# Token-mixing sum of the first layer in two pieces, paired masks in one GpSimd instruction, and another order

## The chip, the cores and the metric

The kernel runs on one core of a Trainium2 chip. The metric is device time in microseconds, as the median of several executions. The profile is one such execution, taken by the hardware profiler.

A core has TensorE (PE; matmuls from SBUF into PSUM), VectorE (DVE), ScalarE (ACT), GpSimd (POOL, which works on SBUF alone here) and SyncE (SP, which issues all DMAs here). Each engine executes its own list of instructions in order and waits on semaphores for the others.

## What is computed

Two layers, each an attention block and a token-mixing MLP, over x of 2048 tokens by 512 channels in bf16. Attention has 32 heads of 16 channels, and a query sees itself and the 255 tokens before it. The MLP mixes over tokens: its sum over s has 2048 terms, its hidden size is 1792.

```python
def _A_ref(x, wqkv, wo):                       # H = 32, Dh = 16, W = 256
    q, k, v = qkv[0], qkv[1], qkv[2]           # from x @ wqkv
    scores = einsum("bhqd,bhkd->bhqk", q, k) * (Dh ** -0.5)
    mask = (i - j >= 0) & (i - j < W)
    p = softmax(where(mask, scores, -1e9))
    return einsum("bhqk,bhkd->bhqd", p, v) @ wo
def _B_ref(x, w1, b1, w2, b2):
    h = layernorm(x)
    u = gelu(einsum("bsd,sf->bdf", h, w1) + b1)
    return transpose(einsum("bdf,fs->bds", u, w2) + b2)
for layer in range(2):
    x = x + _A_ref(layernorm(x), wqkv, wo)
    x = x + _B_ref(layernorm(x), w1, b1, w2, b2)
```

## The kernel before, in words

**Graph and order.** The kernel first describes its work as a graph of some two thousand operations, each with an engine (or alternatives), the tiles it reads and writes, and a cost. Costs and priorities were used by a planner that isn't in the file; what is in the file is its outcome, the text `ORDER`. `replay` goes through it: each entry names the next operation and which of its alternatives (for an eviction, VectorE or ScalarE; for a product, GpSimd or VectorE) is taken. `ORDER` thereby fixes the list of every engine, of the DMA queue too, and which buffer each tile gets. `emit` then writes the instructions and the waits. So whenever the graph changes, a new `ORDER` is needed.

**Units.** A token block is 128 tokens (16 of them, t0 to t15); attention counts in blocks of 64. Channels are worked in four groups `o` of eight heads.

**Attention.** A layer's queries are cut into chunks (`CHUNKS`, L336). Layer 0 has chunks 0 and 1 of four 64-token blocks, then 2, 3 and 4 of eight; layer 1 has four chunks of eight. For every head group a plan (`attention_plan`) lists score steps: which key blocks against which queries, and which columns need a mask. A step is: score matmuls on PE (L673, into two PSUM pairs), two exponentials on ScalarE (L688, PSUM to `pt` in SBUF), the masks on GpSimd (L698, or L700 for a step of two head groups: a multiplication of `pt` by columns of the table `ldm`, seen as int32), and the product with V on PE (L716), which waits for masks. After a head group, VectorE transposes the sum (L736), takes reciprocals (L740), GpSimd or VectorE multiplies (L742), and VectorE transposes back (L747). In a full chunk of eight blocks there are five steps a head group with 1, 2, 2, 2 and 2 masks; a mask of two 64-blocks has 2 x 128 elements a partition, a mask of one has 2 x 64. GpSimd also does the layer norms' power (L485) and part of the K layout (L596).

**Between chunks.** `prepare` brings the layer norm, transposes and Q, K, V of the next 512 tokens. `wo_block` is the output projection of a finished chunk; the residual is added (L758), and the layer norm of those tokens follows (L469 to L492), which makes `xh` of these blocks.

**The MLP's first product** needs all 2048 tokens, so it can't be finished before attention; but part of the sum can be made as soon as some token blocks are normalised. `u_part(s0, s1)` sums over blocks s0 to s1-1: for each of 14 feature tiles of 128, a PSUM group of s1-s0 matmuls (each of 512 columns, L515), then an eviction into an fp32 array (`uA`, which lies in the places of w2b and uT). The first piece is copied there (L822 on VectorE or L824 on ScalarE), a later one is added on VectorE (L826). Every matmul of a piece waits for `xh` of its last block, s1-1 (L820). `PARTS` (L337) lists the pieces: in layer 0, blocks 0 to 3 after chunk 2, 4 to 7 after chunk 3 and 8 to 11 after chunk 4; in layer 1, 0 to 7 after chunk 2 (whose chunks are numbered from 0 too). `u_last` (L837) does the rest, blocks 12 to 15 in layer 0 and 8 to 15 in layer 1, adds what was kept (L848), and ScalarE makes the gelu (L852).

**Weights.** w1 comes through four buffers of 512 KB (`load_w1`, L772). A piece of n blocks loads 2048/n features in a buffer: four tiles for a piece of four blocks, seven for one of eight, with 14 and 28 DMAs of 128 KB. The loads of a piece are put behind the last scores of the chunk before it (`gate`). w2 follows through buffers of `pt` and w2b (L784).

**The MLP's second product** (`y_block`) is 14 matmuls a token block, then the residual (L864); layer 0's blocks are also filler for layer 1's first chunks. In-order PE runs score and value steps, with other matmuls (projections, `u_part`, `y_block`) in between as fillers.

Of the kernel before, what the change touches and what calls it, by code (L numbers as in the profile page):

```python
# [14 lines left out]
ORDER = (
    'c-qZYF^KEP86Mf=-',
    '8q;89q3>JDkh)<9jMR)6$&VzfC36Aph5u^Djaa(LWK(z4mh9#1va3<g%4af;KGFq2Yldwi&waC;lhQBEnK*8V2dqWY~ce3w#cttd+mMi-sW=TA',
    'phHEk7oWE{qz0b|NUkNA?$ljh9bvF5_m$s?}rGvn(I4`qbVll?{q`g-',
    '?_|nUDQY#iel9sb_ZS29uDDs81W$3Zsd6&o7}LuRaZStbu`YoIOW+*p68yo(`CG6x}K%m^>THew~hH+*WZUNX1k-',
    'NY%!CuT2)VT)>Lep!CqFa$t<wa^g-1Ot)=ViPQAklU#nbMDx!Iqn|sdn$3wyxn>^INa-',  # L20
    '3+nS}s;gX8)E^gvR5^csv%Ps;len1WePYX1Ck@@HYX^f;>0cMwZ>tG)-N1Gt-',
    '+?rItCX*Th<_Mk8t%8tmxxR2C#+Gm4CkZCkmOPt`0RZpC+>>w4PK7K=ujX>lCat%0R!wOHG$T&<!=Q5ubgL>E|c99a&(lp{H0OerkSZ;Xt|lB6',
    'oDEYs$LL8?zSy{)!&KQj!&v@BDW2SyYrUDq{2<JT?GlK~T^OOhnZx=vxMVXRb1=6hX{ab+rFCNm}-',
    '4sv_B++`V8=gof(1_OC3%MxS8g0VQ(HA(t*^d0`aqv)n>sv-w0Ih+L}F3U=!DvHcEciY-Vtja4HY^LMSyBOQ_?}w413@Gj49w8)(`ZUb*PPdcO',
    'n`RSZ)6Bb0s$0}c)5_Ob95+a<=G5UkCcn$-',
    'X<f1$$*%i;&98z*aE9Z!J<^qJdyx_=Bg7KLwb8w~xdGsHQ4|%m@OG5YQIr{XX+;ALd_|;n2b1qHk>vY(Syokb+36hS)#&!K<uZ=vkTX%FwB7c<',
    'Gfcfj;T-xmN)-;cQ}uAb2qPp(e64VLPpH5jIlp~R$b{fW2#V}}*&QIXU86NZt6{snZ1;NeS(eQynxUp`+rv($-',
    '9~x0+r^a90dApY6CoADu@MU5I@~x2fDdsEPOB+O6zv|U?t~n`CP+ufu`yOPPt#PX*Oe@jo2JR3><H#EB0y%>6&z7^U5m@2iGU_l5=ACTsz?#$o',
    'M_{E9r8w$YL&A)LL^BLMN<S)NOZlH*Ibt9ZZVzC#0sToI3J+?2%#=Qw^?@6>Ev04Py<#Pv57E61m2ydjkupszvfziSOJk!RaH_9>O8BpD5A?HM',
    'hi5X1);dbh#}gSk<|q*B2CjZ!z6K>>2)1TDQOWOqLzX{;-)8=7GJUD;wC4quS%U*5@iuCWSW79Jl%^DT@Q3!hmz3>lSRe%0ZlrDBP4`zLn-pI-',  # L30
    '@}KZEEchCk~Z*%&h;$IEX^cOhPvG^>V=UO7D=^I0Uev#_GZ|3-',
    'G(iK$RW;=z>3VUdb3$In_(zPe(aC3G?jsdY{inK>ZDl^{2{4sf{nG?Z5Uc_rH$TztIzB8yTVl3QWS*N>qcxrt<LhEbz>PoM9qfG;>2h)FvTjef',
    'rU{d8>V2p1O!b3Aw*n-Fn9ytZ(3DsS?q8)AV&9l6nt+UJm#6-n-',
    'UfE$$mL|2mI<IIC!z>13(?H>>p(EFV}O2jfOvnYX{#Kq;DlE%k<U&VZJr~411_ffn5LzHpIsR&`wqVgb3MeHj;GM-',
    '`?IHmV3r_?EW6~@g9wbccQozHyc?tHW{ePYNZ&4g80{yAsdWFqhHW|x7PzPFbBqP(CZ-~<9GP4q|<G+x`#vF8GMHB@-(G1A&W(;1!-',
    'x4sHXjXf7(mak=bdXK8Rks*#!21T+$XeQJS_at8UKcW@g*XECm*-',
    '7U(_VY0y?$t*Bm&0JS6u!@#e*^_mw&>XgWC7=^VWnlJ!F{^F)#7%sP4D3!JCIM%JbvhVJeaGCksFy7DS^A7u(DYe?L+pV={Ri!!}4~HYKI*OF(',
    'bUGY6lW`dSDp(pzrLWEx%VB@e@6RSm56HjUjfRu$bh6*GZnxL%ZV<|#^1Z<G2A&rrN#cFuiEg!;B+W2Mq9|!55E=sMk4(i#xW-',
    '+x5&J&zL!Z*v>q2^>$cm~I`io&u8(Jze5$k+|(9Mly$vemD?{<d+)F(m$QlY$wNMP4+Jfw6Dn68#&xgw0rkU0Gk0R-UI>-',
    'P$JBuSdy6d!~2I%(oKrnnBxtl0uy26fOSU5|Cs^gR!GfURR!A1rR!mgjXm3Ja!Eh=GI((n;{~u#X=ecDvo<<0F842>1IaI!OCE5=D2pSaLpLvK',  # L40
    'cEgW>h!2&Y7IIZ}R31%d$R$9J4$Zb3i14LT)vit;Qdvq75M*RjVO%SSl)@1l0E}M{yj3Slle=D=Gxb(9OO;ly3wdxk9g7$gzN&W^%uU2n%c=M9',
    'kPIPy0}eBIprCiL$$&W0VxdUL&?+;ZA!58s6_W+!&>~>oxr(a@|1Tw(Zy)XfVWbzYjgZ03n=X=&`ES7%?PinyJ7~63N%4dMxo+m2`$(2NjtRHy',
    'UTscnpobT6H8QO(t&LAn=1`Hk;}CVv*11l+gQWK`$k5wI;)EtH0^Yl;JR#ciRucAfP>HJCrv`hEc~rc~TR#u&D*&d$muI({?<!PKe3Oz$A&+Fb',
    'M0n0?i6T%d%|AR4w35%e4$bIaerxaz*ef18|1kS13$j=qH%)WBml-zuRy&{J~f_omaF_NX7Z&GAjO#R{r#f*X7e<`RsN5GAbRvu3kT1x|gp?xO',
    '8=O`L1&L#s6hP={OWF&Ol}1`IJiWSGn*kouLw*K1u>yuXJ246_*u+rxBco&l@jZ2T))vJcTU0PSO)f!Z{DeSG|nN@K8QMTg+ejl|DqU^n}E#>5',
    'CgYLr^@IPGFQyQ=d5SB39wJUpQ^NjQJd!fX<8(gpb&EbQI2;pCCQq@aEfpeme(ziOTDh5B!Bw5ectqN;qcsxbNb=N5`MzLjQx4%a_&k(b8$~!O',
    'GRE?-RA45U-',
    'xAwR8n6yh0a+SSp=(`CLbpQmIm@Tow&fVKGxwV+mEB*DFtj2@m9H`RFDT{{*3O%*HeHxUiEt9S0cdR(Pda#}$~ohM{npz}MH;$Kmz00EK&vpOm',
    'DGU#K8lpJ-l&YYJz0ic7-G)eA(09Krt!$cp7l?4F*lDy5g@;-',
    'ZBJRn9{6JXN`fzVcQYOD_ZlMJm0b@Uf0dmyABrv$$%3!Uc<8su@r%mxY%)IP$q%08suEk$y0;QmKqyE7Avo22<rH!{rycJWF=zsH>$Pkg8J+zR',  # L50
    '}Qxx4Pg*olyAk&GS>WD4cao_(%gUqJ4IIS-4O~;lyd-;)TMwaXh;UKS3qlRKJgX1mW%LqO<1xZ1VOWqkc10FG`I5f9>A{1U6g'
)
# [259 lines left out]
def bass_interleave_layers__sliding_block__mixer_token_mlp__prompt_kernel(  # L312
# [25 lines left out]

    es = ExitStack()
    with es:  # L340
# [110 lines left out]
        for i, m, c in ((1, 1.0, 0.0), (2, -1.0, 1.0), (3, -1.0, 1.0)):
            op("vector", lambda e, i=i, m=m, c=c: e.tensor_scalar(ldm[:, i, :], ldm[:, 0, :], m, c, op0=ALU.mult, op1=ALU.add),
               reads=["ld0"], writes=[f"ld{i}"])
# [193 lines left out]
        def attention(qs, nq, tqs, tks):  # L647
# [6 lines left out]
            for o2 in range(0, 4, 2) if nq == 4 else range(4):  # L654
# [8 lines left out]
                for su in order:  # L663
# [26 lines left out]
                            ACTF.Exp, scale=SMSCALE), reads=[ts, "acttab"], writes=[(tp, i)], cost=act_cost(2 * cols))  # L690
                    keys = [(tp, 0), (tp, 1)]
                    n = len(su)
                    for c0, nc_, w0 in plan[su[0][0]][1]:
                        def f_mask(e, tp=tp, n=n, c0=c0, w=nc_ * 64, w0=w0):
                            v = probs(tp).bitcast(dt.int32)[:, :, c0 * 64:c0 * 64 + w, 0]
                            msk = ldm[:].rearrange("p a b -> p (a b)")[:, w0 * 64:w0 * 64 + w].unsqueeze(1)
                            if n == 1:
                                return e.tensor_tensor(v, v, msk.to_broadcast([P, 2, w]), op=ALU.mult)  # L698
# [1 line left out]
                            return e.tensor_tensor(v, v, msk.unsqueeze(1).to_broadcast([P, 2, n, w]), op=ALU.mult)  # L700
# [240 lines left out]
```

## Time and profile before

| what | us |
|---|---|
| median of 13 runs | 471.14 |
| lowest and highest | 468.18, 473.12 |
| the profiled execution | 468.32 |
| its span | 466.6 |
| busy: PE, DVE, ACT, POOL | 420.1, 319.4, 325.3, 239.6 |
| exponentials of layer 0, first to last | 11.9 to 166.4 |
| exponentials of layer 1, first to last | 223.6 to 383.0 |

Busy time is what an engine spent in instructions. [...]matmuls overlap, and PE's busy time is not the time in which it can't take more. A group line has the kernel's line, the engine, the operation, output and inputs with their shapes, the count, the busy time in us and the mean in ns of one, and the idle time of the engine before these instructions with what ended it. The groups that bear on the masks and the sum are these:

| line, engine | what | count | mean ns |
|---|---|---|---|
| L688 ACT | exponentials | 304 | 1045 |
| L698 POOL | masks of one head group | 272 | 666 |
| L700 POOL | masks of two head groups | 4 | 1283 |
| L826 DVE | a kept sum read, added to and written | 28 | 677 |
| L822 DVE, L824 ACT | first piece copied | 23, 5 | 685, 600 |
| L736 DVE | output of a head group transposed | 32 | 1246 |

### The profile page before, as it was taken

How to read it: one execution, taken by the hardware profiler on the slowest of the kernel's cores; microseconds unless marked ns; L12 is line 12 of the kernel's file. 1: busy time of each engine (PE TensorE's matmuls, PEld its weight loads, DVE VectorE, ACT ScalarE, POOL GpSimd, SP SyncE). 2: the span in 40 equal slices, each digit the busy share in tenths (PEclk: the TensorE clock that was granted, in tenths of full speed). 3: DMA queues.
4: the chain of work that ended last, by engine and by line, in shares of the span. 5: the costliest groups of instructions: out<-in, count | busy, mean ns of one | idle time of the engine just before them, and what ended most of it. 6: DMA issues, size and time to landing. Idle time of an engine off the chain costs nothing.

```text
span 466.6 us, 14699 instructions
## 1 busy us (share of the span) xinstructions
PE 420.1 (90%) x6383; PEld 200.5 (43%) x6438; DVE 319.4 (68%) x600; ACT 325.3 (70%) x380; POOL 239.6 (51%) x362
## 2 busy tenths in 40 slices
PE   6998899997886798999999989787798989999996
PEld 5764444453332243444454444343333334444442
DVE  6899988788777788445765678786886477530224
ACT  2999999999999931701789889999999981340000
POOL 4578775778587651000335677968996761000000
PEclk8999999999999999999999999999999999999999
DMA  8161531410020347513154000150010437663335
GB/s 251 34 126 38 95 89 34 123 43 1 3 80 25 83 116 205 159 50 87 35 109 103 3 14 4 35 149 4 2 48 24 126 93 200 179 174 96 102 103 163
DMA packets 79392, 39.77 MB, mean 85 GB/s; under 512 B 20960, under 2 KB 79328, under 8 KB 79328
## 3 DMA queue, kind: packets, MB, share of 16 engines
q1 hardware_dynamic: 79328, 38.82, 31.3%
q8 instruction: 51, 0.84, 0.8%
q14 instruction: 13, 0.11, 0.1%
HBM read 33.56 MB, written 2.10 MB: 76 GB/s over the span
## 4 chain that ended last, share of the span: by engine, by line
PE 50%; POOL 17%; ACT 17%; DVE 9%; issue 2%; DMA 2%; SPq 1%
PE PS L515 30%; ACT pt L688 17%; POOL pt L698 14%; PE PS L837 7%; PE PS L716 4%; PE PS L673 4%; PE PS L610 3%; DVE rl L736 2%; PE PS L517 2%; DVE xh_sb L492 2%; DMA x_sb<-in_A_x_dram 2%; POOL kbd L596 1%; POOL ul L742 1%; DVE qT L573 1%; DVE stats L469 1%
## 5 line engine op out<-in xcount | busy, mean ns | idle before, releaser
L688 ACT ACTIVATE pt<-PS 128x1024 bf16<-128x1024 f32 (+1 forms) x304 | 281.8, 1045 | 17.1 <-PE PS L673 15.8
L698 POOL TENSOR_TENSOR pt<-pt,ldm 128x256 int32<-128x256 int32 (+1 forms) x272 | 176.3, 666 | 65.1 <-ACT pt L688 58.7
L515 PE MATMUL PS<-xh_sb,w1b 128*128 128x512 bf16 x258 | 65.2, 380 | 5.5 <-issue 2.4
L673 PE MATMUL PS<-qT,kbd 32*128 32x256 bf16 (+4 forms) x1488 | 60.4, 252 | 7.3 <-ACT pt L688 3.3
L485 POOL TENSOR_TENSOR rstd<-rstd,mhalf 128x2 f32<-128x2 f32 (+1 forms) x33 | 22.7, 690 | 85.3 <-DVE rstd L483 85.3
L515 PE MATMUL PS<-uT,w2b 128*128 128x512 bf16 x250 | 62.5, 379 | 0.8 <-issue 0.6
L515 PE MATMUL PS<-xhT,wqkv 128*128 128x512 bf16 (+1 forms) x234 | 56.9, 372 | 2.2 <-issue 1.8
L716 PE MATMUL PS<-pt,vb 64*32 64x320 bf16 (+4 forms) x2976 | 45.5, 253 | 14.4 <-POOL pt L698 13.2
L864 DVE SCALAR_TENSOR_TENSOR x_sb<-PS,b2col,x_sb 128x512 bf16<-128x512 f32 x32 | 23.4, 747 | 50.8 <-PE PS L515 48.8
L736 DVE STREAM_TRANSPOSE rl<-PS 128x1024 f32<-128x1024 f32 x32 | 39.9, 1246 | 22.4 <-PE PS L716 21.8
L673 PEld LDWEIGHTS PS<-qT,kbd 32*128 32x128 bf16 x1488 | 21.9, 92 | 62.7 <-ACT pt L688 46.0
L852 ACT ACTIVATE uT<-rl,b1col 128x512 bf16<-128x512 f32 x28 | 18.2, 712 | 41.1 <-DVE rl L848 41.0
L469 DVE BATCH_NORM_STATS2 stats<-x_sb 128x6 f32<-128x512 bf16 x64 | 42.3, 678 | 1.4 <-DMA x_sb<-in_A_x_dram 0.8
L716 PEld LDWEIGHTS PS<-pt,vb 64*32 64x32 bf16 x2976 | 28.8, 89 | 33.4 <-POOL pt L698 22.6
L515 PE MATMUL PS<-uT,pt 128*128 128x512 bf16 x163 | 41.4, 379 | 0.3
L492 DVE TENSOR_SCALAR xh_sb<-x_sb,agg,rstd 128x512 bf16<-128x512 bf16 x64 | 33.6, 541 | 9.2 <-POOL rstd L485 9.2
L837 PE MATMUL PS<-xh_sb,w1b 128*128 128x512 bf16 x164 | 37.4, 379 | 2.2 <-issue 2.0
L515 PEld LDWEIGHTS PS<-xh_sb,w1b 128*128 128x128 bf16 x276 | 22.6, 97 | 35.0 <-issue 7.4
L610 PE MATMUL PS<-wqkv,xhT 128*64 128x256 bf16 x512 | 34.0, 275 | 3.6 <-DVE rl L736 1.8
L515 PEld LDWEIGHTS PS<-uT,w2b 128*128 128x128 bf16 x258 | 24.2, 98 | 29.5 <-issue 2.1
L515 PEld LDWEIGHTS PS<-xhT,wqkv 128*128 128x128 bf16 x244 | 21.2, 100 | 25.7 <-issue 5.8
L515 PE MATMUL PS<-wo_sb,oT 128*128 128x512 bf16 x106 | 27.6, 380 | 2.7 <-ACT pt L688 1.2
(64 smaller groups left out, 383.9 us busy)
## 6 DMA issues: line engine op xcount, KB each, us to landing
w1b<-in_B_w_dram SPq DMA_DIRECT2D x112, 128.0 KB, 2.7
w2b<-in_B_w_dram SPq DMA_DIRECT2D x70, 128.0 KB, 2.5
pt<-in_B_w_dram SPq DMA_DIRECT2D x42, 128.0 KB, 3.0
out_dram<-x_sb SPq DMA_DIRECT2D x16, 128.0 KB, 1.8
x_sb<-in_A_x_dram SPq DMA_DIRECT2D x3, 512.0 KB, 6.8
wqkv<-in_A_wqkv_dram SPq DMA_DIRECT2D x4, 256.0 KB, 4.7
wqkv<-in_A_wqkv_dram SPq DMA_DIRECT2D x1, 512.0 KB, 5.5
wo_sb<-in_A_wo_dram SPq DMA_DIRECT2D x1, 512.0 KB, 4.4
```

Source lines behind the costliest of these rows:

```text
L469: op("vector:stat", lambda e: e.bn_stats(stats[:, t, :], x_sb[:, t, :]), reads=[f"x{t}"], writes=[f"st{t}"], cost=dve_cost(512), after=lat ...
L485: op("gpsimd:rstd", lambda e: e.tensor_tensor(rstd[:, t0:t1, 0], rstd[:, t0:t1, 0], mhalf[:, 0:1].to_broadcast([P, t1 - t0]), op=ALU.pow), ...
L492: f_xh = lambda e: e.tensor_scalar(xh_sb[:, t, :], x_sb[:, t, :], agg[:, t, 0:1], rstd[:, t, :], op0=ALU.subtract, op1=ALU.mult)
L515: return e.matmul(o, lhsT=w, rhs=x, start=start, stop=stop, skip_group_check=True)
L610: last = e.matmul(bank(ft)[64 * j:64 * j + 64, sc * 256:(sc + 1) * 256], lhsT=xhT[:, tx.slot, c, tok:tok + 64], rhs=wqkv[:, c, 1024:1536]. ...
L673: last = e.matmul(bank(tt[r // 2], r % 2)[:, base + c0 * 64:base + (c0 + n) * 64], lhsT=kbd[32 * r:32 * r + 32, tk.slot, o, jj].rearrange( ...
L688: op("scalar:exp", lambda e, ts=ts, tp=tp, i=i, cols=cols: e.activation(probs(tp)[:, i, 0:cols, :], pair(ts)[:, :, 0:cols].rearrange("p r ...
L698: return e.tensor_tensor(v, v, msk.to_broadcast([P, 2, w]), op=ALU.mult)
L716: last = e.matmul(bank(t, h)[32 * r:32 * r + 32, i + q0 * 64:i + (q0 + n) * 64], lhsT=vb[64 * h:64 * h + 64, tk.slot, jj, 4 * o + r, :], r ...
L736: op("vector:od", lambda e, t=tod, tr=tr: e.transpose(rl[:, tr.slot:tr.slot + 2].rearrange("p a b -> p (a b)"), pair(t)), reads=[(tod, i) ...
L837: last = e.matmul(bank(tu, tt), lhsT=v()[:, sc - b0, k0 + tt * P:k0 + (tt + 1) * P], rhs=xh_sb[:, sc, :], start=(sc == b0), stop=(sc == NT ...
L864: op("vector:resy", lambda e: e.scalar_tensor_tensor(x_sb[:, t, :], bank(ft), b2col[:, t:t + 1], x_sb[:, t, :], op0=ALU.add, op1=ALU.add), ...
```

## The change

Three things. `PARTS` of layer 0 loses a piece: blocks 0 to 3 are summed after chunk 2 as before, and blocks 4 to 11 in one piece after chunk 4. In a step of one head group, two masks of the same width that follow each other in the plan become one GpSimd instruction, which goes over both column ranges with a step (negative where the second uses earlier columns of `ldm`). And `ORDER` is another text, for the new graph, so the order on every engine, and the choice among alternatives, can differ anywhere.

```diff
 ORDER = (
-    'c-qZYF^KEP86Mf=-',
...
+    'c-qBQKZxtd9iFkZxjC2z^I#5iFb4`Kph5u^I#8hl9jNdF1$3Z72MV}Q;X;K96I3{$!i54Z6ma2U3kO^{;6i~7IN-to7cN}5*kTJ8Te#T5#Rj(6',
...
-    PARTS = [[(2, 0, 4), (3, 4, 8), (4, 8, 12)], [(2, 0, 8)]]
+    PARTS = [[(2, 0, 4), (4, 4, 12)], [(2, 0, 8)]]
...
-                    for c0, nc_, w0 in plan[su[0][0]][1]:
-                        def f_mask(e, tp=tp, n=n, c0=c0, w=nc_ * 64, w0=w0):
-                            v = probs(tp).bitcast(dt.int32)[:, :, c0 * 64:c0 * 64 + w, 0]
-                            msk = ldm[:].rearrange("p a b -> p (a b)")[:, w0 * 64:w0 * 64 + w].unsqueeze(1)
-                            if n == 1:
-                                return e.tensor_tensor(v, v, msk.to_broadcast([P, 2, w]), op=ALU.mult)
-                            v = stepped(v, n, half)
-                            return e.tensor_tensor(v, v, msk.unsqueeze(1).to_broadcast([P, 2, n, w]), op=ALU.mult)
-                        op("gpsimd:mask", f_mask, reads=keys + LD, writes=keys, cost=100 + 2.03 * 2 * n * nc_ * 64)
+                    masks = list(plan[su[0][0]][1])
+                    while masks:
+                        c0, nc_, w0 = masks.pop(0)
+                        reps, cs, ws = n, half, 0
+                        if n == 1 and masks and masks[0][1] == nc_:
+                            c1, _, w1 = masks.pop(0)
+                            reps, cs, ws = 2, (c1 - c0) * 64, (w1 - w0) * 64
+
+                        def f_mask(e, tp=tp, w=nc_ * 64, c0=c0 * 64, w0=w0 * 64, reps=reps, cs=cs, ws=ws):
+                            v = stepped(probs(tp).bitcast(dt.int32)[:, :, c0:c0 + w, 0], reps, cs)
+                            m = ldm[:].rearrange("p a b -> p (a b)")[:, w0:w0 + w]
+                            part, col = [list(a) for a in m.ap]
+                            m = bass.AP(m.tensor, m.offset, [part, [0, 2], [ws, reps], col])
+                            return e.tensor_tensor(v, v, m, op=ALU.mult)
+                        op("gpsimd:mask", f_mask, reads=keys + LD, writes=keys, cost=100 + 2.03 * 2 * reps * nc_ * 64)
```

More of the change, by code (lines that the diff above doesn't have):

```diff
@@ L15 @@
 ORDER = (
-    'c-qZYF^KEP86Mf=-',
[L17 to L50, printed above, removed]
@@ L51 @@
-    '}Qxx4Pg*olyAk&GS>WD4cao_(%gUqJ4IIS-4O~;lyd-;)TMwaXh;UKS3qlRKJgX1mW%LqO<1xZ1VOWqkc10FG`I5f9>A{1U6g'
+    'c-qBQKZxtd9iFkZxjC2z^I#5iFb4`Kph5u^I#8hl9jNdF1$3Z72MV}Q;X;K96I3{$!i54Z6ma2U3kO^{;6i~7IN-to7cN}5*kTJ8Te#T5#Rj(6',
+    'VvGFjUGMY0x9{$92f2~$o%zil{r-I4H;V{D{+|-!d9n0ICvjRfl_V56j?-{lPa=|Oo2F@5X1`bVzV?({@*3#=-',
+    'gWQYyStVUvD1u|_}aEMzHhI5;kdd38x+Mf)umW0gt92h`Aib>b#J@97M0vtOIK*IIA1N6E2e2dS+YP=Svz1(k_ZuojuSGuX~_+jG4KQF44R{9A',
+    'w1ez__FI>xg2b?C<w9b^NxJeY2TH!YxVvd7i+Ovig2|`7v9y?{7SIP^;G7pqVPKQMV4jb$;I{Pa=W>%D$~@)hNewfuju(b%W8BicbOJ>nx^r^#',
@@ new lines @@
+    'dMl@x<1w>i6+c3W8-',
+    't(>#j7<&CrrM_F9PZf%9fG$a7A3k`%>%itNp~tbuFpX48yB6p3(~reP2Su@Ec4!m!DLTfd^d&w1ffw`A=69D*ztlZnerJGX7uwODF;x}o}-',
+    'syoiNZo}0ZGY{fbth+mE(1(YITg$e@RrZy(-',
+    'fnM9%TysVD>0k>Lnvl7rX$mk4VfxLa9LH~Xm@w|?QNo{s@SO8t1CG74`QLr=c>BfO>Zcb$z&oSne%(fmdho(-',
+    'R)R;Q*O8Y{`RJ9H@h49m)y%QeK)$A&z;4hF>^Qbc6**)etkKc(dlxvlq6}fSUy+}%jM#Br6}+NM_n&B(|=vkf797?O{Y`&pG$c$9?!?)ao@hE?',
+    '2Fv)R28MeAsvmYs1s$Q;WW>w86;_zqO@Q32YskUchl{rDK%QqcSLH7*56v+(;hWA=MMK~%(EMcrY-',
+    'l#Q@r0!FH{ve3Rl^eG61(f>i4PVc_n=F!t-DzYdfOLx#u@bv(aF-9R!s6hrXc-',
@@ new lines @@
+    '*$n_?mk(>z_cVmAu6!RE55C1Hr3@a3Yz*m=WuugNp=&zlnwo^6Zt&3a;1Er2d#-',
+    '8NR(WT0uIr}f7>x#h!+6R#CrEmLlS&OLMEHjD%N>%*R_2Q>Ws6HOU(M%2sG4e3cU4tQI3bMCid11Wr-',
+    'X!eb3#5JRNYA@&q;^3dCEnb5X~?&poAI|$9Dj9gm58-',
+    '`>hu0nYpPFi3v%DN)cbm2ZIRMAQ`srx8lG@p690lkUv9V)QoKhX+fjW_43%z1xgZvRLHPkZAJ)ED3K{+oCukaUT;K)EtL1;7>>^KBuP+WS=N4t',
+    'goMn4ASen@XR**mqbW!TN49OtiU~P{5^`B<wPelX!0j)@mwO8fpg8O;Wt!{ct(JCsYh-',
+    '$y8X}D%O>Kse%9Pu8jBnpIJjVtKby+UprQ<O`#J2|hmWbo7VStbsP;g<}j77Gs>w3dxiei|WW(vj-xcC;y5@#yVN>eFCii*(XV!d9^W@w7UlmT',
@@ new lines @@
+    'qz$!IWER)fJvQIK?dTb6C4Qz{{;FJvEDPeDkQ!&Vq8Xf>I9r+nx0=$$H$dP9&fL6(FAZ0;ZnJB5(VHQ8NnB0IFdS>vUrsuG`0Igp}4{EeYOG!7',
+    'koK1RIX@B3$EiNY|1oM^q|j96B-',
+    '$eN#<*!N@XU5^k70@U}R+=16Aiexqk4*h1U88_1`@L_M@w;FC)x=I1LvKx&sY=lv0%OLxds092+H#=#!dw77IU+*jlU2kXCtJw_rVoa)PG--',
+    '}*cDuM~AVx294dg~sp&8UPq%LGV>#kN^K#b86%jB!SpBDpwyrgHzo)d~9y(8cHx3|DabJJ|T`zBmQAksq2=e?OB8EPc+FOp<3%(BG!k|(2w*>E',
+    '_}+=>R7;SL?u9u3FC!TFF7VgaNj=>iQN-uBCKbTb@5Ns7x$&<QU3eCoOvyy!Z^`(e>577LH_?!|b_%^|ni?Ve#kwc;SELO<|*H*Pgso)@`1iXz',
@@ new lines @@
+    'X`V+}ZzYHxLwQOMhk0k}27Ad!eEo4R>F*KcLbb#={AEb>>`G)kcpS<7=>V{N3h+fk}%#`ivfi%d~u8xg>jWPw)S-',
+    'vQkzA{+zWR_j%#*8#~aiq1tft7g;bwCY|^I_c0snqsrx-?Yj$JS)?T<G3BS+wFpM({|eJf~OIQn(&)9-',
+    'sM1lIzVs%bbumAA|wvgFccy|h=;O#2X7<1VY(0ZNJ8#`Yl?Dn6DfGHTr8LKJuTNWyRs(}I~GXp_hmFZAHuS{Uk(Po%QIfURn;ppf`YUq%gs2Zk',
+    'S^-Tn#`1KxOE)+%I4zt`tO9bB0{3#LT2O1+cOC<oFjx$ny%6+U9`vP8j`?~fe;9ZKnMwR*@>FF-',
+    'I7Ke9BdVnaSI(9R4327e$nh^VKdzS2hbRfhVX%ik`#2>1oDNxxj<?&)+$+zP-$m8@Z7?f84V|~WoBw-',
+    'r(+np#dLO~6XW_C^0*gpNkN=JHEe04BFicPK*e-w7{;bR*)EehgF#1(vQ;+J_rB!ac5LVSCaf$*u{InIQNbqOc<g0<5O#oJVS}-',
@@ new lines @@
+    'D&p%Jqz9jWTI&0_Nx^i1^*-1w3bUKj@`9}r>g5XltKyNsw{Ln1U4JyO^j($nQ9~tlmL;PgKKX3{N_>aEha0bR8ekbNS-',
+    'v9Xw;p04*K0|v8!u9?9<I=t9*nb+<PhL<%zp2$~C&L%5_Q80+{5Vsu!>5kUz;^by?(A{Jet^%;jysN7sn<@TdYqM>;;TJ|bXZxd9TM^s@;+jGJ',
+    'OsZ?`##`$9lu_Sk4l4oYz?@5>c_!SL$BtecATpn;(gj%d%x;%Q0>uY7~n@2@zc*^c=*F2|B!?Dr-HIx|J2~;wa17defSXXp%Aqievw)H>?8gF`',
+    'gk8`4L@?=z3u4Ud(NCv2fs?E54eT!|CX0ut-',
+    'V@;C&+w+ujiE4KIY!@cwdUzEBL@4BnLm1=CKO+Wlp72c|spTvVIDj`tzuM095@D(v$7c@XFdxC!zLAGCna?JG9rPYagQmzd*zxc<H2%CHx+ihg',
@@ L52 @@
+    'dOwNkRN1#h@uK<ES4KQa{*Frs^*$@M$ofz1(qH+M4ttB<TnMNjkvb@G=lv33TxkF}0`M?4Rer$!S544n64*e&*$gn>G9z1doWRokWE({>5CYeZ',
+    '=bbI&rKLKK1{l#GK3@fsK#FJSr?cxhS5b96w78MlU<B$t?ca0{n_vVRWL6zedA9)rfyy)c=>T{tJ-WI_&'
 )
```

## The prediction

> **What bounds the kernel now.** I read the slices of the span first, then the chain that ended last, then busy times by stage, then the groups of POOL and VectorE by shape, and last the stretch in which layer 0's attention hands over to its MLP.
>
> ```profile
> PE   6998899997886798999999989787798989999996
> ...
> ACT  2999999999999931701789889999999981340000
> POOL 4578775778587651000335677968996761000000
> ...
> PE 50%; POOL 17%; ACT 17%; DVE 9%; issue 2%; DMA 2%; SPq 1%
> ```
>
> ScalarE is at 9 tenths wherever attention runs (slices 2 to 14 and 20 to 32) and nearly empty between; there TensorE carries the time. So there are two regimes: attention, paced by 304 exponentials, and the MLP, paced by matmuls. The chain is half PE, with POOL and ACT at 17% each: the POOL share is the masks of L698, which stand between an exponential and the product with V.
>
> The starts of the exponentials (12, 20, 40, 40, 40 in layer 0, then 32, 40, 40, 40) cut the span into its chunks:
>
> ```profile
> 46.40:88.00 41.60, 38.15 (x761) 17.99 (x764) 35.66 (x69) 39.73 (x45) 29.76 (x46) 1.00 0.32 70
> 88.00:128.30 40.30, 35.29 (x729) 15.87 (x734) 32.80 (x58) 38.12 (x43) 29.07 (x42) 1.00 0.15 41
> 128.30:166.40 38.10, 30.15 (x644) 12.37 (x644) 28.50 (x48) 37.27 (x41) 29.28 (x44) 1.00 0.22 61
> 166.40:178.60 12.20, 9.97 (x135) 4.43 (x135) 11.01 (x21) 1.57 (x2) 3.59 (x5) 1.00 0.62 170
> ...
> 264.00:305.30 41.30, 36.03 (x720) 17.35 (x724) 31.52 (x51) 38.30 (x42) 34.27 (x51) 1.00 0.08 18
> 305.30:342.60 37.30, 30.44 (x706) 13.84 (x704) 29.21 (x60) 37.02 (x41) 30.62 (x47) 1.00 0.17 46
> 342.60:383.00 40.40, 37.33 (x678) 15.34 (x679) 27.08 (x46) 37.39 (x41) 29.69 (x44) 1.00 0.28 79
> ```
>
> Columns: stretch, length, busy PE, PE loads, DVE, ACT, POOL, clock, DMA. The first four rows are chunks 2, 3, 4 of layer 0 and the hand-over; the last three are the later chunks of layer 1. A run of ten exponentials takes 9.28 us on the chain, so 40 need 37.1 us. Chunk 4 (38.1) and the third of layer 1 (37.3) are at that floor. Chunks 2 and 3 lie 4.5 and 3.2 us above it, 7.7 together; the second and last of layer 1 lie 4.2 and 3.3 above. That is what a better attention could give.
>
> [...]
>
> ```profile
> L698 POOL TENSOR_TENSOR pt<-pt,ldm 128x256 int32<-128x256 int32 x192 | 139.6, 738 | 42.8 <-ACT pt L688 39.0
> L698 POOL TENSOR_TENSOR pt<-pt,ldm 128x128 int32<-128x128 int32 x80 | 39.4, 496 | 22.3 <-ACT pt L688 19.7 <-DVE ldm L452 1.1
> ...
> L700 POOL TENSOR_TENSOR pt<-pt,ldm 128x768 int32<-128x768 int32 x2 | 3.6, 1814 | 1.0 <-ACT pt L688 1.0
> ...
> L700 POOL TENSOR_TENSOR pt<-pt,ldm 128x256 int32<-128x256 int32 x2 | 1.5, 752 | 0.0
> ```
>
> From 752 at 256 to 1814 at 768 elements is 2.07 ns each, with some 220 ns left for the instruction. [...]L826's 28 adds take 675 to 679 here. [...]the table gives a 512-column matmul 379 ns, yet the chain shows 49 of them in 10.74 us, 219 ns apart. I price TensorE work at 219. [...]
>
> **The change, part by part.**
>
> *Masks.* In a full eight-block chunk, each of four head groups has two steps whose pair of masks becomes one: 8 merges. Counted over the plans: 48 in the six such chunks, 8 in layer 1's first chunk, 4 in layer 0's first; 60 in all, 52 of 256+256 elements, 8 of 128+128. A merged large one: 752 + 256 x 2.07 = 1282 ns against 2 x 738 = 1476, so 0.19 us saved; a small one: 2 x 496 - 752 = 0.24. Sum 52 x 0.19 + 8 x 0.24 = 11.8 us of POOL. The new form strides the mask backwards, which no row shows. Low bound: no saving, if the walk costs as much as a second dispatch; a loss is unlikely, since the four-dimensional 256 row costs only 14 ns more than the plain one. High bound 0.25 each, 15 us. I take 0.19. What reaches the path: chunks 2 and 3 hold 16 merges, 3.0 us, against 7.7 us over the floor, and their chain hops between masks and exponentials. I let the 3.0 pass. In layer 1 the second chunk has POOL busy 34.3 of 41.3 us and 4.2 over the floor: 8 merges, 1.5 us, pass; the last chunk has fewer masks on the chain and I take half, 0.8. Chunk 4, layer 1's third (at the floor) and its first (PE 39.6 of 40.4 us busy) give nothing. Sum: 5.3 us less.
>
> *Adds.* One of three read-add-write passes over the 14 feature tiles goes: 14 x 0.68 = 9.5 us of VectorE, between 116 and 148 us. VectorE is busy 32.8 of 40.3 and 28.5 of 38.1 us there, so this is no bound; ScalarE hides it. It makes the layer norm of token blocks 8 to 11 quicker, which the next part needs. By itself 0; high bound 1 us, if evictions that ScalarE does (3 of 0.6 us in chunk 2, 2 in chunk 3) go to VectorE.
>
> *The sum moved.* Matmuls don't change in number. But L820 makes every matmul of a part read the normalised block s1-1. Blocks 4 to 7 could start once block 7 was there (first matmul 114.3 us); now they wait for block 11, whose normalisation ended at 152 us. So 56 matmuls, 56 x 0.219 = 12.3 us, leave chunk 3 and early chunk 4, where PE can be idle behind ScalarE at no cost, and join the other 56 after it.
>
> ```profile
> 107.00:145.00 38.00, 11.80 (x46) 3.83 (x50) 1.00 0.09 26
> 145.00:152.00 7.00, 1.86 (x8) 0.63 (x8) 1.00 0.14 40
> 152.00:167.00 15.00, 8.56 (x35) 2.95 (x36) 1.00 0.31 83
> 167.00:178.60 11.60, 4.45 (x20) 1.77 (x20) 1.00 0.60 165
> ...
> 360.00:370.00 10.00, 6.41 (x28) 2.37 (x29) 1.00 0.32 86
> ```
>
> These are matmuls that read w1b (busy PE in the third column, their count beside it). Beside attention they went at 35 in 15 us, 2.3 a us; the best stretch of layer 1 has 2.8. Block 11 need not be as late as 152: chunk 3's last transpose of the output ran at 131.1 us, and what follows is some 8 us of VectorE work amid attention's share of a third, so about 145. From 145 to the last exponential at 166.5, at 2.8 a us, 60 of the 112 are done. 52 remain, 11.4 us, with 16 matmuls of the last output projection, 3.5: 14.9, so the last piece starts at 181.4 and not 178.6: **+2.8 us**. The bounds: start at 143 and 3.2 a us, +0 (75 done); start at 152 and 2.3 a us, 33 done, 79 x 0.219 + 3.5 = 20.8, +8.7.
>
> *Weight loads.* 14 DMAs of 128 KB leave the time before 128 us and follow chunk 3's last scores, with rows of 512 B in place of 1 KB. SP's queue then holds 14 more ahead of the last piece's 14 and the w2 loads; 1.8 MB at the 170 GB/s of 166 to 178 us is 11 us of transfer, hidden by 128 to 152 us with DMA below 0.2; without it the last piece would wait that much. In return the eight-block weights come in 7 tiles, so the last piece gets its buffers earlier: the chain's wait for w1b at 174 to 178 us should go. It lies within the time counted above; 0.
>
> *New order.* It can move every instruction; its cost can't be read from the page. I take 0 with 3 us either way: the idle time of ScalarE inside attention is what it can win.
>
> Sum: -5.3 + 2.8 = -2.5 us. The profiled execution took 468.3 us (span 466.6 and 1.7 around it): 465.8. It is 2.8 below the median 471.1 of 13 runs, so on the median's footing **468.6**.
>
> **The rivals.**
> (1) *Saved work is hidden.* The merged masks pass a third of their 5.3 us, and the sum costs its 2.8: +1.0, 472. For: ACT is over 0.9 in all chunks, and the POOL pieces on the chain may only be the neighbour of a saturated engine. Against: 13.2 us of PE and 22.6 of its loads waited for masks.
> (2) *The cover is gone, slower.* The one mechanism: PE runs short in chunk 3 and the 112 matmuls start only when block 11 is normalised; TensorE becomes the bound from there. At a start of 152 and 2.3 a us +8.7, less 3.7 for masks that pass: +5, 476. It decides if the first eight-block matmul starts after about 149. For: the kernel before ended block 11 at 152 with the same reductions pending. Against: nothing had pressed for it, as blocks 4 to 7 filled PE.
> (3) *The order gains more.* All 7.7 + 4.2 + 3.3 us over the floor but a third are recovered, 10, with +2.8: -7, 464. For: VectorE and POOL both have slack to give. Against: of the six full chunks above, only two sit at the floor.
> That the change doesn't do what it says is excluded, but for the order.
>
> **How the numbers follow.** About 0.3%, 1.4 us, is what a measurement of this kernel can tell from no change. Chances: the forecast 0.42, (1) 0.18, (2) 0.28, (3) 0.12. Of the forecast's share, 0.04 falls within 0.3%, and 0.04 of (1) falls outside on the slow side: faster 0.50, same 0.18, slower 0.32. The range, 462.5 to 476.5, takes in (1), most of (2) and most of (3); the faster cases alone run from 462.5 to 469.7.
>
> **What would show it.** Masks: 128x512 rows on POOL near 1280 ns, 216 mask instructions, POOL some 12 us less busy; 1450 or more kills that step. Adds: 14 rows of L826, not 28. The sum: no w1b matmul from 86 us to about 145, then 112 in a row, last piece beginning near 181; later than 184 is rival (2). ScalarE: chunks 2 and 3 of layer 0 at 79 us together where they were 81.9. The forecast is wrong if the hand-over slips by more than attention gains.

## The result, and the profile after

The changed kernel takes 463.04 us in the median (462.28 to 465.29, 11 runs); the kernel before took 469.72 in all its runs by then (48). The ratio is 0.986, 95% interval 0.9839 to 0.9881: about 6.6 us faster. The prediction had 468.6 against 471.1, 2.5 faster, with a range of 462.5 to 476.5. The direction holds and the time lies just inside the range's fast end, so more than twice as much came as the steps say. The profiled execution has a span of 460.8 us against 466.6.

The slices of PE, ACT and POOL and the chain by engine, from the page of the changed kernel:

```profile
PE   6998787998777999999999999998789999999996
...
ACT  6997789999989960616988898999979962340000
POOL 3668678677866651000466557676956661000000
...
PE 61%; ACT 15%; DVE 12%; POOL 7%; issue 3%; DMA 1%; SPq 0%; POOLq 0%
```

POOL's share of the chain falls from 17% to 7%, and PE's rises from 50% to 61%. PE is now at 9 tenths from slice 14 through slice 27 without a break; before, the row has 7 at slice 14, 8 at slice 16, and 7s and 8s again from slice 24. So the work of TensorE is spread differently around the join of the layers. The masks by shape, from POOL's groups after:

```profile
L705 POOL TENSOR_TENSOR pt<-pt,ldm 128x256 int32<-128x256 int32 x98 | 73.2, 752 | 42.3 <-ACT pt L687 37.8 <-DVE ldm L451 2.6
L705 POOL TENSOR_TENSOR pt<-pt,ldm 128x512 int32<-128x512 int32 x52 | 66.8, 1287 | 23.8 <-ACT pt L687 23.4
```

A merged mask takes 1287 ns; the prediction worked out 1282. The stretches of the changed kernel, cut as those of before at its own exponentials (length, then busy PE, PE loads, DVE, ACT, POOL, clock, DMA):

```profile
43.70:86.40 42.70, 35.09 (x773) 17.04 (x772) 37.66 (x65) 37.59 (x41) 30.87 (x41) 1.00 0.30 64
...
126.10:167.40 41.30, 35.22 (x660) 14.45 (x659) 27.50 (x49) 37.62 (x42) 27.64 (x35) 0.92 0.32 87
...
215.30:249.90 34.60, 33.91 (x577) 17.55 (x581) 22.63 (x42) 32.05 (x40) 18.51 (x25) 1.00 0.38 74
249.90:294.60 44.70, 42.45 (x738) 19.63 (x750) 34.61 (x67) 39.75 (x45) 26.48 (x33) 1.00 0.21 46
```

These are chunks 2 and 4 of layer 0 and the first two of layer 1. The line of before for layer 1's first chunk, which the prediction quotes but doesn't show:

```profile
223.60:264.00 40.40, 39.61 (x611) 20.56 (x609) 26.82 (x57) 34.85 (x43) 18.46 (x32) 1.00 0.31 67
```

Most attention stretches are not shorter than before: chunks 2 and 4 take 42.7 and 41.3 against 41.6 and 38.1, the second of layer 1 takes 44.7 against 41.3, and its last two take 39.8 and 41.7 against 37.3 and 40.4. One gains much: layer 1's first chunk takes 34.6 us, where before it took 40.4. Points of both traces, in us from the span's start (starts and ends of exponentials, and one matmul; the stretches above are cut some 0.3 us earlier):

| point | before | after | difference |
|---|---|---|---|
| chunk 1 of layer 0 ends | 46.9 | 42.4 | -4.5 |
| chunk 3 ends | 128.8 | 126.3 | -2.6 |
| chunk 4 ends | 166.7 | 167.7 | +1.0 |
| last matmul of layer 0's first product begins | 192.9 | 192.8 | -0.1 |
| layer 1: first exponential | 223.9 | 215.6 | -8.3 |
| its first chunk ends | 264.0 | 250.1 | -13.8 |
| second | 305.7 | 294.5 | -11.3 |
| third | 343.0 | 334.3 | -8.7 |
| fourth | 383.2 | 376.4 | -6.8 |

At the end of layer 0's attention nothing is won: the 4.5 us of its first two chunks are spent by then. The gap between the layers' attention, from the last exponential of layer 0 to the first of layer 1, then falls from 57.2 to 47.9 us. By the end of layer 1's first chunk 13.8 us are won, and half is given back. What differs there is where layer 0's second product lies. PE's loads for matmuls that read uT, first before, then after:

```profile
178.60:210.00 31.40, 8.71 (x90) 1.00 0.45 127
210.00:250.00 40.00, 8.71 (x107) 1.00 0.32 77
250.00:306.00 56.00, 3.80 (x50) 1.00 0.14 31
```

```profile
178.60:210.00 31.40, 7.33 (x76) 1.00 0.50 140
210.00:250.00 40.00, 5.62 (x74) 1.00 0.33 65
250.00:306.00 56.00, 7.07 (x84) 1.00 0.25 59
```

Before, 197 of these loads come before 250 us and 50 after; in the changed kernel 150 and 84, as late as 305 us. Some matmuls are made in halves, with two loads. In whole matmuls, 224 in all, 136 ran before layer 1's first exponential, 78 beside its first chunk and 10 beside its second; in the changed kernel 84, 56 and 56, and 28 beside its third. The 52 that no longer stand ahead of layer 1 are 11.4 us at the 0.219 us that the prediction uses. Before, the whole product was done at 268 us; PE was busy 39.6 of the 40.4 us of layer 1's first chunk, and in its next chunks 36.0 of 41.3 and 30.4 of 37.3. The new order spreads this work over what had been idle.

### The profile page after: what moved, and what is told of

Its sections match the earlier page's. It is cut to its first block, busy times and chain, and to the rows that moved or that the text cites. A ratio compares the mean times of both kernels' runs of the same rounds, so it can differ in the third digit from the quotient of the medians.

```text
span 460.8 us, 14645 instructions
## 1 busy us (share of the span) xinstructions
PE 418.9 (91%) x6394; PEld 200.7 (44%) x6456; DVE 323.6 (70%) x596; ACT 325.9 (71%) x377; POOL 226.9 (49%) x296
## 4 chain that ended last, share of the span: by engine, by line
PE 61%; ACT 15%; DVE 12%; POOL 7%; issue 3%; DMA 1%; SPq 0%; POOLq 0%
PE PS L514 36%; ACT pt L687 14%; PE PS L842 8%; POOL pt L705 6%; PE PS L672 6%; PE PS L721 6%; PE PS L609 3%; PE PS L516 3%; DVE rl L741 2%; DVE xh_sb L491 2%; ACT kbd L582 1%; DVE kbd L595 1%; POOL rstd L484 1%; DMA xhT<-xh_sb 1%; DVE qT L572 1%
## 5 line engine op out<-in xcount | busy, mean ns | idle before, releaser
L705 POOL TENSOR_TENSOR pt<-pt,ldm 128x256 int32<-128x256 int32 (+3 forms) x216 | 171.0, 807 | 89.4 <-ACT pt L687 83.5
L484 POOL TENSOR_TENSOR rstd<-rstd,mhalf 128x2 f32<-128x2 f32 (+1 forms) x33 | 23.9, 726 | 63.5 <-DVE rstd L482 62.2
L514 PE MATMUL PS<-xhT,wqkv 128*128 128x512 bf16 (+1 forms) x198 | 46.4, 356 | 5.4 <-ACT pt L687 2.2
L672 PEld LDWEIGHTS PS<-qT,kbd 32*128 32x128 bf16 x1488 | 22.0, 92 | 67.0 <-ACT pt L687 44.7
L491 DVE TENSOR_SCALAR xh_sb<-x_sb,agg,rstd 128x512 bf16<-128x512 bf16 x64 | 37.0, 594 | 7.3 <-POOL rstd L484 7.1
L514 PE MATMUL PS<-uT,pt 128*128 128x512 bf16 x165 | 39.8, 379 | 0.2
L609 PE MATMUL PS<-wqkv,xhT 128*64 128x256 bf16 x512 | 36.0, 276 | 0.8 <-DMA xhT<-xh_sb 0.4
L514 PE MATMUL PS<-wo_sb,oT 128*128 128x512 bf16 x109 | 29.0, 393 | 2.0 <-DVE xh_sb L491 1.0
L609 PEld LDWEIGHTS PS<-wqkv,xhT 128*64 128x64 bf16 x512 | 25.0, 109 | 9.8 <-issue 4.5
```

What stands on the lines that cost most here:

```text
L484: op("gpsimd:rstd", lambda e: e.tensor_tensor(rstd[:, t0:t1, 0], rstd[:, t0:t1, 0], mhalf[:, 0:1].to_broadcast([P, t1 - t0]), op=ALU.pow), ...
L491: f_xh = lambda e: e.tensor_scalar(xh_sb[:, t, :], x_sb[:, t, :], agg[:, t, 0:1], rstd[:, t, :], op0=ALU.subtract, op1=ALU.mult)
L514: return e.matmul(o, lhsT=w, rhs=x, start=start, stop=stop, skip_group_check=True)
L609: last = e.matmul(bank(ft)[64 * j:64 * j + 64, sc * 256:(sc + 1) * 256], lhsT=xhT[:, tx.slot, c, tok:tok + 64], rhs=wqkv[:, c, 1024:1536]. ...
L672: last = e.matmul(bank(tt[r // 2], r % 2)[:, base + c0 * 64:base + (c0 + n) * 64], lhsT=kbd[32 * r:32 * r + 32, tk.slot, o, jj].rearrange( ...
L705: return e.tensor_tensor(v, v, m, op=ALU.mult)
```

## The experiments

Every kernel is compared with the kernel before, which was run anew beside each batch. Its median there lay between 468.5 and 471.0 us, so it is the ratio that counts, and microseconds are worked out from it. The expectations name the theories, A to D. An order was made from the two that were given: the operations of the graph are matched by what they do, so that one kernel's sequence can be laid on the other's graph. An operation whose inputs or buffers aren't there yet goes as soon as they are. Line numbers shift by some lines from kernel to kernel.

### Masks, in either order

Only the masks merged, in the kernel before (the second mask of a pair leaves `ORDER`):

```diff
-                    for c0, nc_, w0 in plan[su[0][0]][1]:
+                    masks = list(plan[su[0][0]][1])
+                    while masks:
...
```

> The kernel before with the paired masks merged, each merged mask at the place of the first of its pair, and nothing else (three pieces of the sum, the order of before). Theory A (the gain is the order of layer 1's beginning; the masks lie beside ScalarE): 0 to -1 us against before. Theory B (the prediction's step: 5.3 of 11.8 us of POOL pass to the path): -4 to -5.5 us. POOL should be some 12 us less busy under both.

466.73 us, ratio 0.9956 (0.9929 to 0.9983): 2.1 us faster. That is neither theory A nor B.

The other way round, the changed kernel with pairs split:

```diff
-                        if n == 1 and masks and masks[0][1] == nc_:
+                        if False and masks and masks[0][1] == nc_:
```

> The changed kernel with every merged mask split into its two again, the second straight behind the first; two pieces of the sum and the new order stay. Theory A: within 1 us of the changed kernel, so about -6 against before. Theory B: slower than the changed kernel by 4 to 5.5 us, so about -1.5 against before.

470.56 us, ratio 1.0015 (0.9996 to 1.0033). Without merged masks the whole gain is gone. Against the changed kernel (1.0015 / 0.986) the masks are worth 1.6%, 7.3 us. Theory A, that they lie beside ScalarE, falls; theory B had 4 to 5.5, too little here and too much in the old order, where they are worth less than a third of 7.3. Who waited for whom gives a first answer. First the kernel before, then the one with merged masks alone, then the changed kernel with its masks split, then the changed kernel (us in total, times, longest):

```profile
PEld PS L716 <- POOL pt L698: 22.6, 31, 1.6
ACT pt L688 <- PE PS L673: 15.8, 33, 1.3
```

```profile
ACT pt L679 <- PE PS L664: 17.2, 32, 2.1
PEld PS L713 <- POOL pt L697: 13.6, 25, 1.5
```

```profile
ACT pt L679 <- PE PS L664: 30.1, 43, 2.4
PEld PS L713 <- POOL pt L697: 24.2, 35, 1.7
```

```profile
ACT pt L687 <- PE PS L672: 24.0, 37, 2.4
PEld PS L721 <- POOL pt L705: 14.0, 26, 1.4
```

With the waits of the matmuls themselves (13.2, 5.0, 12.0 and 5.4 us more), merging takes some 17 us from PE's waits for masks in both orders: 35.8 to 18.6, and 36.2 to 19.4. In the old order ScalarE's waits for scores stay (15.8, 17.2): an exponential was hardly ever late because of PE's wait. In the new order they fall from 30.1 to 24.0. The reading is that TensorE has more to do beside attention there, so that what it loses at a mask comes back as a late score. Chunk by chunk, from first to last exponential, the split kernel is longer than the changed one by 0.8, 1.0, 1.0 and 0.2 us in chunks 1 to 4 of layer 0, and by 0.7, 1.0, 2.5 and 0.7 in layer 1, 7.9 together. A part of the 2.5 is the clock: over this chunk the granted clock was 0.96 in the split kernel (299.8 to 341.7 us) and 1.00 in the changed one (294.6 to 334.4 us).

### The order, in either layer

Layer 1's new order on the kernel before, and layer 0's new order with layer 1's old one:

```diff
-ORDER = (the order of before)
+ORDER = (operations of one layer as before, of the other as in the changed kernel)
```

> The kernel before (three pieces, plain masks) with its own order for layer 0's operations, and the changed kernel's order for everything that is counted to layer 1, the second product of layer 0's MLP included. Theory A: -5 to -7 us against before, as first exponential of layer 1 and y blocks move as in the changed kernel. Theory B (masks and sum, not the order): within 1.5 us of before.

468.34 us, ratio 0.996 (0.994 to 0.9981): 1.9 us faster. The first exponential of layer 1 starts at 215.3 us, as in the changed kernel, and its first chunk ends at 253.3 (before 264.0), but the next chunk takes 45.4 us, and most is given back. Theory A's 5 to 7 us don't come from the order alone.

> The changed kernel (two pieces, merged masks) with its own order for layer 0's operations and the order of before for layer 1's. Theory A: within 1.5 us of before, since layer 0 ends at the same time in both traces (last addition to the first product at 193.6 and 195.3 us). Theory B: -2.5 to -5 us, since masks are merged in both layers and the sum is in two pieces.

471.6 us, ratio 1.0035 (1.0017 to 1.0054): slower, although it has merged masks and the two pieces. Beside merged masks alone (0.9956) the new layer 0 loses 0.8% when the old layer 1 follows. Neither theory had that; A's bound of 1.5 us is just missed, B's gain is out. The trace shows where it is lost: layer 1 starts at 229.7 us (225.6 with merged masks alone) and then takes as long, 158.0 us of exponentials against 157.8. The gap between the layers takes 60.1 us where it took 57.0, with the same 136 matmuls of the second product in it. When the last matmul of the first product began, only 4 of them had been issued and not 10.

Now merged masks and layer 1's new order, but layer 0 as it was, in three pieces:

> The kernel before in layer 0, order and three pieces of the sum included, the changed kernel's order in layer 1, and merged masks in both: everything of the change but the sum in two pieces and layer 0's new order. Theory C (masks and layer 1's order are worth more together than apart; the sum in two pieces gives and costs nothing): 462 to 465 us, -5 to -7 against before, like the changed kernel. Rival D (two pieces and the layer 0 order made for them are part of the gain): 466 us or more, -1 to -4.

463.96 us, ratio 0.9853 (0.982 to 0.9886), like the changed kernel's 0.986. This is the run that decides: theory C. Apart, masks give 2.1 and layer 1's order 1.9 us; together they give 6.9. The sum in two pieces and the new order of layer 0 are not needed for it.

Why more together than apart? The four kernels with layer 0's old order, in us of their traces:

| | old order, plain | old, merged | new order of layer 1, plain | new, merged |
|---|---|---|---|---|
| kernel | before | masks_alone | layer1_after | three_pieces_merged |
| gap between the layers' exponentials | 57.2 | 57.0 | 47.2 | 47.0 |
| layer 1, first to last exponential | 159.3 | 157.8 | 166.9 | 162.8 |
| of it ScalarE waiting for scores | 10.7 | 9.7 | 17.8 | 14.3 |

The new order wins 10 us in the gap, with plain masks and with merged ones. It pays for them in layer 1's attention, where much of the second product now lies: 7.6 us with plain masks, 5.0 with merged ones. So merged masks save 1.5 us there in the old order and 4.1 in the new, and of these 2.6 us more, 2.5 are ScalarE's waits for scores. These are single traces, but the times come again: 159.3 us in the kernel with the sum alone and 158.0 in that with layer 0's new order (old order of layer 1, plain and merged), and 164.7 and 160.7 where both layers have the new order. Over both layers the waits are 23.6 us in the third kernel and in the fourth. The trace of the fourth is of the longest of its six executions, 467.1 us, and it is layer 0 that is longer in it (attention ends at 171.3 us), so the waits over both layers can't show this.

### The sum

In the kernel before, `PARTS` alone, with the eight-block piece at the places of blocks 8 to 11:

```diff
-    PARTS = [[(2, 0, 4), (3, 4, 8), (4, 8, 12)], [(2, 0, 8)]]
+    PARTS = [[(2, 0, 4), (4, 4, 12)], [(2, 0, 8)]]
```

> The kernel before with layer 0's blocks 4 to 11 summed in one piece, its matmuls, evictions and loads at the places that blocks 8 to 11 had; plain masks, order of before otherwise. The prediction's step (56 matmuls of 12.3 us lose their cover; start bound by block 11, here at 152 us, with no order made for it): +2.8 to +8.7 us against before. Rival (chunk 4 has room for them behind ScalarE): 0 to +1.5 us.

492.64 us, ratio 1.044 (1.039 to 1.0491): 20.7 us slower, over twice the upper expectation. Its last stretches of layer 0 (columns as above):

```profile
128.00:150.00 22.00, 14.90 (x320) 5.25 (x312) 11.11 (x21) 19.43 (x22) 15.43 (x24) 0.73 0.27 73
...
172.00:190.00 18.00, 12.31 (x137) 4.64 (x136) 4.70 (x8) 1.09 (x1) 2.37 (x3) 0.91 0.39 109
```

Two costs show that the prediction didn't price. The granted clock is 0.73 where it had been 1.00; chunk 4 takes 44.6 us (before 38.1). And from 172 us PE waits for weights, 8.0 us in all, as on the chain:

```profile
173.14 2.56 DMA w1b<-in_B_w_dram
...
183.84 2.71 DMA w1b<-in_B_w_dram
```

The seven tiles and the last piece's four share four buffers, and in the old places a load goes out only when a tile is used up. The cover itself: the piece begins at 152.6 us, and when chunk 4 ends 60 of its matmuls are left where 19 of the old last part were. These 41 are 9.0 us, just over the prediction's high bound. So the loss is the piece in an order not made for it, and not the cover alone.

The additions by themselves: the changed kernel with its eight-block piece made as two of four, one after the other for each feature tile, with 14 more additions.

```diff
-    PARTS = [[(2, 0, 4), (4, 4, 12)], [(2, 0, 8)]]
+    PARTS = [[(2, 0, 4), (3, 4, 8), (4, 8, 12)], [(2, 0, 8)]]
```

> The changed kernel with the eight-block piece made as two four-block pieces one after the other for each feature tile, in its place; 14 more additions on VectorE, no earlier start, everything else as in the changed kernel. If the additions cost nothing, as predicted (hidden behind ScalarE): within 1 us of the changed kernel, about -6 against before. If VectorE is on the path in that stretch: up to 9.5 us slower than the changed kernel.

483.15 us, ratio 1.0267 (1.0226 to 1.0309): 12.6 us slower than before. This doesn't price the additions, since the edit brought waits of its own. Chunk 4 takes 48.4 us (41.2 in the changed kernel). PE's loads waited 8.5 us for additions to the same array (5.1 in the part at w2b, 3.4 in that at uT; two sums of one tile follow each other) and 4.4 us for w1, from 165 to 200 us:

```profile
PEld PS L506 <- DVE w2b L823: 5.1, 3, 3.0
PEld PS L834 <- DMA w1b<-in_B_w_dram: 4.4, 1, 4.4
```

A bound is theory C's kernel, which makes the 14 additions more and is no slower. But it has layer 0's old order and three pieces as well: dropping the additions, moving the sum and layer 0's new order together make 0.3 us, with 1.9 us of uncertainty, and the additions alone aren't priced.

### Which part of layer 1's order

The second product's late blocks alone, moved in one order to where the other has them:

> The kernel before with one edit of its order: the matmuls and residuals of the token blocks 6 to 15 of layer 0's second product come after as many score steps of layer 1 as in the changed kernel; what depends on them follows as soon as it can. Theory A1 (it is this postponement alone): first exponential of layer 1 6 to 9 us earlier, -4 to -7 us against before. Rival A2 (it needs the whole new order of layer 1, as projections, transposes and buffers were placed for the old one): -2 to +3 us, with the early start given back in the chunks that follow.

533.23 us, ratio 1.1307 (1.1247 to 1.1366).

> The changed kernel with the token blocks 6 to 15 of layer 0's second product at the places, counted in score steps of layer 1, that they had in the kernel before. Theory A1: the gain is gone, within 2 us of before, with the first exponential of layer 1 near 223 us. Rival A2: half or more of the gain stays, -3 us or better against before.

532.06 us, ratio 1.13 (1.1255 to 1.1344). Both are useless as tests of the size. ScalarE waits for scores 40.0 us in the first two chunks of layer 1 of the one and 49.9 of the other (before 7.7). The likely reason is that layer norms, projections and evictions had been placed for the old positions and here follow all at once; it wasn't tested apart. In the first kernel layer 1 does start at 217.2 us, 6.7 earlier, but its first two chunks take 62.7 and 72.9 us. A gentler shift, in which few operations had to follow:

> The kernel before (plain masks, three pieces) with the token blocks 10 to 15 of layer 0's second product put later in its own order: blocks 10 and 11 by some four score steps of layer 1, 12 to 15 by six to ten, so that 12 to 15 lie beside its second chunk and not its first; what depends on them follows when it can. If TensorE's overload in the first chunk of layer 1 is what the new order cures: first chunk ends 5 to 10 us earlier and -2 to -5 us against before. If the later chunks have no room: 0 to +3.

488.12 us, ratio 1.0378 (1.0333 to 1.0423). The first chunk ends at 269.2 us, later than before, and the second takes 56.2. Again ScalarE waits for scores (26.2 us from 223 to 330, before 7.7), presumably behind what depends on the late blocks.

Last, a cut: layer 1's two orders joined at the 43rd of its 76 score steps, with merged masks and layer 0 as before.

> Merged masks, three pieces and layer 0 in the order of before; layer 1 in the changed kernel's order up to its 43rd of 76 score steps (by which all 16 token blocks of layer 0's second product are done in both orders), then what is left in the order of before. If the gain of the new order lies in the first steps, where those blocks are spread over 42 score steps and not over 18: 462 to 465 us, -5 to -7 against before. If it lies in the later steps: 466 to 468, as with merged masks alone.

473.17 us, ratio 1.0089 (1.0061 to 1.0118). Neither end was met. Up to the join the lead is there: the second chunk ends at 295.3 us (306.7 with merged masks alone). At the join 13 us are lost, since the old order counts on work that the new one does later: the longest of ScalarE's waits for scores is 14.3 us, and in it, from 308 to 324 us, the chain runs through layer norm, the copy of xh and projections for the next tokens. The stretch with the join, 53.2 us where the changed kernel has 39.8:

```profile
295.40:348.60 53.20, 42.16 (x759) 19.04 (x758) 38.19 (x69) 37.88 (x42) 31.63 (x41) 0.94 0.24 49
```

> The complement: merged masks, three pieces and layer 0 in the order of before; layer 1 in the order of before up to its 43rd score step, then what is left in the changed kernel's order. If the gain lies in the first steps: 466 to 468 us, as with merged masks alone. If in the later ones: 462 to 465.

476.62 us, ratio 1.0173 (1.0144 to 1.0203). Here up to the join there is no lead (second chunk ends at 305.6), and the rest loses. So the lead is made in the first steps; that it lives to the end needs the rest of the same order. This is shown for the lead, not for its size at the end. The lead is mostly the gap between the layers: 47.0 to 48.4 us in five traces that begin layer 1 in the new order, 57.0 to 57.2 in three that begin it in the old one behind the old layer 0.

## Why the prediction was right, and where not

**Masks.** Count (60), duration (1282 against 1287) and POOL's saving held: 11.8 was forecast; busy time fell by 12.7, other work included, and the mask groups alone by 10.7 (184.1 to 173.4). What reaches the path was put at 5.3 us: 3.0 in layer 0's chunks 2 and 3 and 2.3 in layer 1. The traces give 2.0 in those two chunks, and 4.9 in layer 1. The term that was too small was for chunks taken to be at the floor or held by PE: layer 1's first chunk gives 0.7 and its third 2.5 (in part by the clock), where none was expected. They were at their limit in the old order only. In the old order 2.1 us pass in all, less than half of the term, and none where 3.0 were expected: chunks 2 and 3 take 42.3 and 40.8 us with merged masks, and 41.1 and 40.5 without. In the new order 7.3 pass. Even there the sign that was named, chunks 2 and 3 at 79 us together and not 81.9, didn't come: it is 82.4, as the new order lost there what the masks saved. The share of a saving that passes belongs to the order, and not to the masks.

**The sum moved.** The last piece was to begin at 181.4 us; it begins at 181.1. But it doesn't get there by the sum that was given. Matmuls that read w1b, 46 beside attention from 152 to 167 us, where 35 had run:

```profile
152.00:167.00 15.00, 11.01 (x46) 4.06 (x50) 1.00 0.44 124
```

The eight-block piece begins at 143.0 us: block 11 was normalised by then and not at 152, a little earlier than the 145 that was argued. At 3.1 a us, near the fast bound, 37 matmuls are left when attention ends, and not 52: 3.3 us less. Attention ends at 167.7 and not 166.5, and 96 value matmuls, 1.4 us that the sum left out, come behind it. So 181.1 is right by errors that cancel. (Blocks 0 to 3 also ran on until 126.8 us, where no such matmul was expected from 86.) The debt is there: at 210 us 14 fewer loads of the second product have been issued, 3.1 us at 0.219, and 16 transposes of 0.055, done by 210.3, stand in their stead, so some 2.2 remain. With layer 1's old order behind it the debt shows: layer 0's new order lengthens the gap by 3.1 us. In the changed kernel it isn't seen at the end, as 52 fewer matmuls stand ahead of layer 1. Theory C's kernel, without that debt but without layer 0's new order too, is 0.3 us faster than the changed one by the ratios, with 1.9 us of uncertainty. So +2.8 is about right where the old order of layer 1 follows, and was wrong for the end of the changed kernel.

**Adds and loads.** The 14 additions are gone; that they cost nothing, as said, fits the runs but isn't shown apart. (Of ScalarE's five evictions that the prediction placed in chunks 2 and 3, two lie in layer 1, at 383 and 388 us; nothing rests on it.) The chain's wait for w1b at 174 to 178 us is gone as well: from 165.9 us on it is TensorE, with holes of 0.16 us at most.

```profile
165.90 2.54 PE PS L514 x11
168.44 1.36 PE PS L721 x76
...
169.96 10.74 PE PS L514 x49
...
181.13 10.36 PE PS L842 x48
```

**New order.** It was given 0, 3 us either way, with ScalarE's idle time in attention as what it can win. This step failed in size and in place. Layer 1's order gives 1.9 us alone and 4.8 with merged masks (0.9956 to 0.9853). And it wins by a thing that the prediction had in its hands and used as a reason for no gain: "its first (PE 39.6 of 40.4 us busy) give nothing". A stretch bound by PE next to stretches where PE had 5 to 7 us to spare is work that can be moved. The gap, in which layer 0's second product ran ahead of layer 1's first exponential, wasn't weighed as something that an order can shorten, and that is where the gain arises. The slices had a sign too: ScalarE isn't at 9 tenths in all of 20 to 32, as was read, but at 7, 8, 9, 8, 8 in slices 20 to 24.

**The rivals.** (1), saved work hidden, describes the masks in the old order only. (2), cover gone, was seen in the eight-block piece without a new order: 9.0 of its 20.7 us are cover. With a new order it was avoided: block 11 came early, and the piece of blocks 0 to 3 was spread out until then. (3), the order gains more, is what happened, at -6.6 against its -7. That the numbers agree is luck, as it doesn't come by the recovery of chunks over the floor that it named: these are longer than before. Luck has a part in the forecast as well. Its direction came true, but its terms of -5.3 for the masks and 0 for the order were both too small, +2.8 isn't seen at the end, and a range of 14 us is wide enough to take in the sum of other terms.

By the ratios, merged masks and layer 1's order together give some 3 us more than apart (the intervals leave 0.8 to 5.2), and layer 1's attention shows 2.6 of them. Open: why merged masks lengthen chunk 2 in the old order; what each part of layer 0's change, the moved sum, the additions and the order, is worth by itself; and how much of the masks' 7.3 us goes by way of the clock.

## What to carry to other kernels

A saving on an engine beside the bound is worth what the order of the queues lets through: the same masks gave 2.1 us in one order and 7.3 in another, so measure it in the order that will be used. Where work of one stage fills another, compare the stretches: one at its limit beside one with room is a candidate that a table of busy times by stage shows. And this order couldn't be mended locally: five edits that moved a few of its operations, with a reason for each, cost 3 to 13%, and two that joined whole orders inside layer 1 cost 0.9 and 1.7%.

## What was not expected of the hardware

In two of these traces TensorE's granted clock was halved behind a stretch in which it had little work. In the kernel with the sum alone, PE was busy 5 tenths of the slice from 109.7 to 121.9 us, where blocks 4 to 7 had been taken out (9.3 of these 12.2 us in the kernel before, whose clock stayed at 1.00). From 118 to 138 us its granted clock was then 0.51 (before 1.00), and from 120 to 240 us ScalarE waited 7.1 us for scores (before 2.7). In the changed kernel the clock was 0.92 over chunk 4, as it was halved twice for 3.4 us, from 131.5 us (0.51) and from 141.7 us (0.50); in the 3.4 us before, PE had been busy for 1.6 and 1.8. The first matmuls of the eight-block piece, from 143.0 us, started 0.43 us apart, and 0.22 once the clock was back. A lack of work isn't all that it takes: in the same trace PE was busy for 1.0 of the 3.4 us from 45.2 us, and the clock stayed at 1.00. What else it takes isn't shown. Filler matmuls beside attention thus seem to have done more than their own work in the kernel before: with blocks 4 to 7 gone, the scores were late too.
